# Attention and SwiGLU block with gradients: the forward loop staggered by one head, three weights transposed by DMA, the backward V loads issued earlier

## The chip, the cores and the metric

The kernel runs on one core of one Trainium2 chip. The core has five engines that run side by side, each in the order in which its own instructions were written: PE (matrix products), DVE (vector work), ACT (scalar work and copies), POOL (more vector work), and SP, which here only issues DMA transfers. Sixteen DMA engines move data between HBM and the on-chip memory. The metric is the device time of one execution in microseconds (us); lower is better.

## The reference

One decode step (batch 4, one token) of a pre-norm block, and its gradients. `_layernorm`, `_silu` and `_softmax` are the usual ones.

```python
def _A_ref(x, k_cache, v_cache, wq, wo):            # H=32 heads, Sk=4096, Dh=128
    q = (x @ wq).reshape(B, Sq, H, Dh).transpose(0, 2, 1, 3)
    p = softmax(einsum("bhqd,bhkd->bhqk", q, k_cache) * Dh ** -0.5)
    o = einsum("bhqk,bhkd->bhqd", p, v_cache)
    return o.transpose(0, 2, 1, 3).reshape(B, Sq, H * Dh) @ wo
def _B_ref(x, w1, w3, w2):                          # D=512, F=1792
    return (silu(x @ w1) * (x @ w3)) @ w2
h  = x + _A_ref(_layernorm(x), k_cache, v_cache, wq, wo)
h2 = h + _B_ref(_layernorm(h), w1, w3, w2)
out, vjp = jax.vjp(f, x, k_cache, v_cache, wq, wo, w1, w3, w2); grads = vjp(grad_out)
```

The outputs are `h2` and the gradients of x, k_cache, v_cache, wq, wo, w1, w3 and w2, in bf16. The two caches hold 128 heads (batch times heads) of 4096x128 values, 1 MB each; their gradients have the same size.

## The kernel before

**Forward.** The loop runs over 64 pairs of heads (`NGI` iterations `gi`, heads `a` and `b_`). For a pair, K is transposed (`T_pe`: one quarter of a head by PE with a copy by ACT, L309 and L310; `T_dve`: three quarters by DVE, L315), scores S are formed by PE (`S_head`, L341), and a softmax follows that passes between engines: row maximum on DVE (`mx` L348), a transpose on PE (`x_ps`), `gm` on DVE, a broadcast on PE (`b_ps`), `nm` on DVE, the exponential on ACT (`E`), the sum on PE (`l_ps` L379), its reciprocal on DVE (`rl` L384), the scaled copy `Pn` on ACT (L387), eight transposes of it on PE (`pt_P` L394) and four copies into `P_all` on ACT (L398). Then POOL writes the probabilities as pairs into a buffer PK (`PK_pairs` L404) and DVE multiplies K by them (`PK_mul` L408). In the next iteration PE forms the product M of V and PK over 32 blocks (`M_mm` L422), the sums `kP` (`M_end` L432) and ACT copies M out (L436). M and kP let the backward pass give the gradient of q without reading K again. Every eighth head ends a group: `wo_load` fetches 256 KB of wo and `attn` adds the attention output to `xr` (`at_ps` L461, L463).

**Buffers and queues.** All large tiles share 21 slots of 1 MB, given out in the order in which they were given back. K is loaded six heads ahead (`KQ`), V three (`VQ`), both by SP. SP's transfers use eight completion semaphores in turn, so an issue also waits until the eighth transfer before it has landed, and whatever stands behind it on SP waits too.

**Middle.** After the last head come the second layernorm (its root on ACT, L226), the products with w1 and w3 (`gu_ps`), the gate (`sigT` on ACT by Sigmoid, L709, and some DVE work), the product `dhn_ps` with w1 and w3 transposed (L724), the layernorm's gradient (L729 to L736), and the product `dOT_ps` with wo transposed (`woT`). The transposes of w1 and w3 (`wT_units`) and of wo (`woT_units`) are made by PE and copied out by ACT and DVE between the other steps; each weight is loaded once, as it lies in HBM.

**Backward.** For each of 128 heads V is loaded again and transposed (L928, L929), dP is formed (L933), and DVE forms the 1 MB gradients gv and gk as outer products (L940), which POOL and SP store. The loads of V for it (`load_V2`) begin in the middle; `prefetch` keeps up to seven ahead. The other gradients are worked off in small pieces beside it (`side_work`).

The core of the loop before:

```python
S_head(gi, 0); S_head(gi, 1); sm_max(gi)            # softmax of pair gi
M_mm(pa, ...)  ... sm_exp(gi) ... M_end(pa)         # M of the pair before
sm_sum(gi); sm_norm(gi)
M_mm(pb, 0, SJ); M_end(pb); load_V(pb + VQ)
T_pe(nb); sm_P(gi); PK_pairs(a); PK_pairs(b_)
PK_mul(a); T_dve(nb, 1..3); PK_mul(b_)
```

Of the kernel before, what the change touches and what calls it, by code (L numbers as in the profile page):

```python
# [9 lines left out]
FP32 = mybir.dt.float32  # L10
BF16 = mybir.dt.bfloat16
ALU = mybir.AluOpType
# [4 lines left out]
KQ = 6  # L17
# [8 lines left out]
def kernel(  # L26
# [116 lines left out]

    for s in range(KQ):
        load_K(s)
# [153 lines left out]
    hold = {}  # L299

# [105 lines left out]
    def PK_mul(s):  # L406
        PK = PKs[s].t[:].rearrange("p (j c) -> p j c", c=PKW)
        nc.vector.tensor_tensor(  # L408
            out=PK[:, :, 0:Dh].rearrange("p j (r t) -> p j r t", t=2),
            in0=Ks[s].heads().rearrange("p j (r t) -> p j r t", t=2),  # L410
            in1=PK[:, :, None, Dh:PKW].to_broadcast([P, SJ, Dh // 2, 2]),
            op=ALU.mult,
        )
        Ks.pop(s).give()

# [50 lines left out]
    def two_slots(nm):  # L466
        return [Slot(nm + "a"), Slot(nm + "b")]
# [7 lines left out]
    def load_w13(ap, nm):  # L475
        sl = two_slots(nm)
        for i in range(2):
            nc.sync.dma_start(out=sl[i].b(2 * F).rearrange("p (c f) -> p c f", c=2),
                              in_=ap[i * 2 * P:(i + 1) * 2 * P, :].rearrange("(c p) f -> p c f", p=P))
        return sl  # L480

# [38 lines left out]
    mid_w = {}  # L520

    def wT_units():
        for nm in ("w1", "w3"):
            w = mid_w[nm]
            wT = two_slots(nm + "T")
            mid_w[nm + "T"] = wT
            for f0 in range(0, FC, 2):
                pt = psT.tile([P, 2, DC, P], BF16, tag="tps", name="pt_w13")
                for i in range(2):
                    for cc in range(DC):  # L530
                        nc.tensor.transpose(pt[:, i, cc, :], w13_view(w, cc)[:, (f0 + i) * P:(f0 + i + 1) * P], ident_b[:])
                for i in range(2):
                    if (f0 // 7) == (f0 + 1) // 7:
                        if i == 0:
                            dst = wT[f0 // 7].b(7 * D).rearrange("p (c j) -> p c j", c=7)[:, f0 % 7:f0 % 7 + 2, :]
                            nc.scalar.copy(out=dst.rearrange("p a (n c) -> p a n c", c=P), in_=pt[:])
                    else:
                        nc.scalar.copy(out=w2_view(wT, f0 + i).rearrange("p (n c) -> p n c", c=P), in_=pt[:, i])
                yield

    units = {"d": d_hh_units(), "w": wT_units()}
# [13 lines left out]
    for gi in range(NGI + 1):  # L555
        fwd = gi < NGI
        last = gi >= NGI - 1
        a, b_ = gi * G, gi * G + 1
        pa, pb = a - 2, a - 1
        na, nb = a + 2, a + 3  # L560
        nxt = na < NH
# [7 lines left out]
        if gi > 0 and pb % 8 == 7:  # L569
            wo_load(pb)  # L570
        if gi > 0:
            M_mm(pa, 0, SJ // 2)
        if nxt:
            T_dve(na, 1)
        if fwd:
            sm_max_T(gi)
            sm_gmax(gi)
        if gi > 0:
            M_mm(pa, SJ // 2, SJ)
        if nxt:  # L580
            T_dve(na, 2)
        if fwd:
            sm_bcast(gi)
            sm_exp(gi)
        if gi > 0:
            M_end(pa)
            load_V(pa + VQ)
        if nxt:
            T_dve(na, 3)
        if fwd:  # L590
            sm_sum(gi)
            sm_norm(gi)
        if gi > 0:
            M_mm(pb, 0, SJ)
            M_end(pb)
            load_V(pb + VQ)
            if pb % 32 == 31:
                kP_flush(pb)
            if pb % 8 == 7:
                attn(pb)  # L600
        if nxt:
            T_pe(nb)
        if fwd:
            sm_P(gi)
            PK_pairs(a)
            PK_pairs(b_)
            PK_mul(a)
            load_K(a + KQ)
        if nxt:
            for c in range(NPE, 4):  # L610
                T_dve(nb, c)
        if fwd:
            PK_mul(b_)
            load_K(b_ + KQ)
        hold.pop(gi - 1, None)
        if 2 <= gi:
            step("d")
        if gi == NGI - 3:
            mid_w["w1"] = load_w13(B_w1, "w1")
        if gi == NGI - 2:  # L620
            mid_w["w3"] = load_w13(B_w3, "w3")
        if gi == NGI - 1:
            step("w", 7)
    step("w", 20)
# [20 lines left out]
    wo_pg = []  # L645

    def load_wo_page():
        pg = len(wo_pg)
        if pg < H // 8:
            wo_pg.append(Slot("wo8"))  # L650
            nc.sync.dma_start(out=wo_pg[pg].heads().rearrange("p j d -> p (j d)").rearrange("p (h j) -> p h j", h=8),
                              in_=A_wo[pg * 8 * P:(pg + 1) * 8 * P, :].rearrange("(h d) j -> d h j", d=P))

# [10 lines left out]
    with ExitStack() as cm:  # L664
# [3 lines left out]
        psWt = cm.enter_context(tc.tile_pool(name="psWt", bufs=4, space=bass.MemoryType.PSUM))  # L668
        for _ in range(4):
            load_wo_page()  # L670

# [4 lines left out]
        hhatT = mid.tile([P, DC, B], BF16, name="hhatT")  # L676
        rows_to_T(psA, hhatT[:], hhat, B, DC)
# [10 lines left out]
        woT = [Slot(f"woT{jj}") for jj in range(DC)]  # L688

        def woT_units():  # L690
            for pg in range(H // 8):
                for jj in range(DC):
                    pt = psWt.tile([P, GW, P], BF16, tag="wT", name="pt_wo")
                    src = wo_pg[pg].b(8 * D).rearrange("p (h j) -> p h j", h=8)
                    for hl in range(8):
                        nc.tensor.transpose(pt[:, hl, :], src[:, hl, jj * P:(jj + 1) * P], ident_b[:])
                    evac_copy(woT[jj].b(HD)[:, pg * 8 * P:(pg + 1) * 8 * P].rearrange("p (n c) -> p n c", c=P), pt[:],
                              eng="v" if jj == 3 else "s")
                    yield
                wo_pg[pg].give()  # L700

        units["o"] = woT_units()
# [6 lines left out]
        nc.scalar.activation(out=sigT[:], in_=gu_ps[:, 0], func=AF.Sigmoid)  # L709
        nc.vector.tensor_copy(out=gateT[:], in_=gu_ps[:, 0])  # L710
        nc.vector.tensor_copy(out=upT[:], in_=gu_ps[:, 1])
        step("o", 3)
# [15 lines left out]
        step("o", 4)  # L728
        nc.vector.tensor_copy(out=d_hn, in_=dhn_ps[:])  # L729
        for _ in range(3):  # L730
            load_V2()
        step("o", 5)
# [4 lines left out]
        step("o", 20)  # L737
# [7 lines left out]
        for h in range(H):  # L745
            for jj in range(DC):
                nc.tensor.matmul(dOT_ps[:, h, :], lhsT=woT[jj].b(HD)[:, h * Dh:(h + 1) * Dh], rhs=dhT[:, jj, :],
                                 start=(jj == 0), stop=(jj == DC - 1))
        for sl in woT:
            sl.give()  # L750
# [259 lines left out]
```

## Time and profile before

| | |
|---|---|
| time, median of 3 runs | 2164.55 us (2160.97 to 2164.81) |
| profiled execution: time, span | 2167.34 us, 2165.2 us |
| busy share of PE, DVE, ACT, POOL | 70%, 58%, 44%, 20% |
| bytes moved, mean rate | 712.01 MB, 329 GB/s |
| first and last row maximum of the forward | 23.3 us, 1045.9 us |
| first gradient product of the backward | 1108.14 us |

The span is the time from the first to the last instruction of the profiled execution; all places in the program below are given in us from its start. A row of the timeline gives start, duration, engine, line, operation, output and inputs, the number of instructions merged, and in brackets how long the engine had been idle and what ended that. PEclk is the granted share of the full TensorE clock, the DMA share the mean busy share of the sixteen DMA engines.

### The profile page before, as it was taken

To read this page: it belongs to the slowest core of one execution; us is meant where nothing else is said; L and a number is where in the kernel's file an instruction comes from. 1 tells how busy PE (TensorE), PEld (TensorE's weight loads), DVE (VectorE), ACT (ScalarE), POOL (GpSimd) and SP (SyncE) were. 2 spreads that over 40 slices of the span, in tenths; PEclk is the share of its full clock that TensorE was granted. 3 is DMA by queue.
4 is the path that set the end of the run, shared out by engine and by line. 5 is a ranking of instruction groups with operands and counts; after the bars stand their busy time and mean duration, and the time that the engine had idled before them with its cause. 6 is when DMAs were issued, how large, how long until landed. Compare 5 with 4: busy or idle time off the path is not lost.

```text
span 2165.2 us, 43701 instructions
## 1 busy us (share of the span) xinstructions
PE 1508.0 (70%) x18905; PEld 1212.3 (56%) x18905; DVE 1265.7 (58%) x1459; ACT 957.3 (44%) x1463; POOL 431.6 (20%) x665
## 2 busy tenths in 40 slices
PE   5767767777776776776788877686478658557553
PEld 4555555555555554555578875565366546446553
DVE  5556556556556556656356655475475666466665
ACT  2333322332232332232455555576377547546553
POOL 2121122122122112112011110121112222123232
PEclk8887887887788888788875666655565555556555
DMA  9876867677676776766589999899999999999998
GB/s 406 294 259 253 321 237 256 239 285 268 235 267 247 272 273 231 282 242 246 208 321 414 418 372 417 373 365 408 387 400 411 410 416 393 391 364 418 409 403 346
DMA packets 116400, 712.01 MB, mean 329 GB/s; under 512 B 11488, under 2 KB 29160, under 8 KB 33264
## 3 DMA queue, kind: packets, MB, share of 16 engines
q1 hardware_dynamic: 97520, 574.96, 69.1%
q0 software_dynamic: 18688, 134.28, 15.1%
q8 instruction: 147, 2.41, 0.4%
q14 instruction: 45, 0.37, 0.0%
HBM read 426.78 MB, written 282.34 MB: 328 GB/s over the span
## 4 chain that ended last, share of the span: by engine, by line
DMA 23%; PE 10%; ACT 9%; DVE 5%; issue 2%; SPq 1%; ACTq 0%; DVEq 0%
DMA out_dram<-gk 19%; ACT VT L929 7%; PE pt_tps L928 4%; DMA wq<-in_A_wq_dram 3%; DVE gv L940 2%; DVE gk L940 2%; PE dq_ps L781 2%; DMA w2a<-in_B_w_dram 1%; SPq L661 1%; PE dP_ps L933 1%; DMA out_dram<-gv 1%; PE gps L775 1%; PE rep_ps L912 1%; ACT rq L915 0%; ACT wqT L812 0%
## 5 line engine op out<-in xcount | busy, mean ns | idle before, releaser
L929 ACT COPY VT<-pt_tps 128x1024 bf16<-128x1024 bf16 x512 | 492.6, 1016 | 196.9 <-PE pt_tps L928 158.8
L928 PE MATMUL pt_tps<-ident_b,V 128*128 128x128 bf16 x4096 | 450.9, 293 | 114.7 <-ACT VT L929 114.7
L928 PEld LDWEIGHTS <-V 128*128 128x128 bf16 x4096 | 398.7, 137 | 174.8 <-issue 157.4
L408 DVE TENSOR_TENSOR PK<-Kn,PK 128x4096 bf16<-128x4096 bf16 x128 | 290.7, 2272 | 269.7 <-POOL PK L404 269.7
L940 DVE TENSOR_TENSOR gv<-P,rdo 128x4096 bf16<-128x4096 bf16 x128 | 293.7, 2295 | 171.6 <-DMA out_dram<-gk 144.8
L940 DVE TENSOR_TENSOR gk<-dS,rq 128x4096 bf16<-128x4096 bf16 x128 | 294.2, 2298 | 109.8 <-DMA out_dram<-gk 95.4
L422 PE MATMUL M_ps<-PK,Vn 128*128 128x130 bf16 x4096 | 344.8, 253 | 0.0
L310 ACT COPY KT<-pt_tps 128x1024 bf16<-128x1024 bf16 x128 | 129.4, 1012 | 468.6 <-PE pt_tps L309 446.7
L341 PE MATMUL S_ps<-KT,W 128*32 128x256 bf16 x1536 | 153.1, 345 | 253.9 <-DVE KT L315 253.9
L422 PEld LDWEIGHTS <-Vn 128*128 128x128 bf16 x4096 | 327.6, 118 | 3.9 <-issue 0.8
L315 DVE STREAM_TRANSPOSE KT<-Kn 128x512 f32<-128x512 f32 x384 | 254.7, 689 | 0.0
L952 POOL DMA_DIRECT2D out_dram<-gv x128 | 68.1, 532 | 837.2 <-DVE dSt L955 587.9
L933 PE MATMUL dP_ps<-dOT_bf,VT 128*128 128x1 bf16 x4096 | 150.2, 166 | 117.9 <-DVE dSt L955 59.2
L341 PEld LDWEIGHTS <-W 128*32 128x32 bf16 x1536 | 69.4, 107 | 287.2 <-issue 282.6
L933 PEld LDWEIGHTS <-VT 128*128 128x128 bf16 x4096 | 139.7, 103 | 132.2 <-ACT VT L929 69.0
L404 POOL COPY PK<-P_all 128x64 bf16<-128x64 bf16 x128 | 26.6, 241 | 819.0 <-ACT P_all L398 819.0
L321 POOL TENSOR_TENSOR W<-qrep,wmask 128x128 bf16<-128x128 bf16 x128 | 179.3, 1400 | 14.4 <-DVE qrep L272 14.4
L936 POOL COPY P<-P_all 128x64 bf16<-128x64 bf16 x128 | 140.7, 1099 | 0.0
L341 PE MATMUL S_ps<-KT,zq 128*32 128x256 bf16 x512 | 108.9, 332 | 4.0 <-ACT KT L310 0.3
L309 PEld LDWEIGHTS <-Kn 128*128 128x128 bf16 x1024 | 79.4, 120 | 54.1 <-issue 52.4
L309 PE MATMUL pt_tps<-ident_b,Kn 128*128 128x128 bf16 x1024 | 107.2, 268 | 0.7 <-DVE qrep L272 0.7
L373 ACT ACTIVATE E<-S_ps,nm 128x256 f32<-128x256 f32 x64 | 30.4, 474 | 173.9 <-DVE nm L370 173.9
(221 smaller groups left out, 1250.9 us busy)
## 6 DMA issues: line engine op xcount, KB each, us to landing
Kn<-in_A_k_cache_dram SPq DMA_DIRECT2D x128, 1024.0 KB, 5.1
Vn<-in_A_v_cache_dram SPq DMA_DIRECT2D x128, 1024.0 KB, 6.7
V<-in_A_v_cache_dram SPq DMA_DIRECT2D x128, 1024.0 KB, 21.8
out_dram<-gv POOLq DMA_DIRECT2D x128, 1024.0 KB, 11.2
out_dram<-gk SPq DMA_DIRECT2D x128, 1024.0 KB, 20.0
wq<-in_A_wq_dram SPq DMA_DIRECT2D x8, 1024.0 KB, 11.1
out_dram<-gw SPq DMA_DIRECT2D x6, 896.0 KB, 22.5
wo<-in_A_wo_dram SPq DMA_DIRECT2D x16, 256.0 KB, 6.4
```

The source lines that it names most:

```text
L309: nc.tensor.transpose(pt[:, i, :], Kn[:, c * GW + i, :], ident_b[:])
L310: nc.scalar.copy(out=KT[:, c * GW:(c + 1) * GW, :], in_=pt[:])
L315: nc.vector.transpose(out=KT[:, c * w_:(c + 1) * w_], in_=Kn[:, c * w_:(c + 1) * w_])
L321: nc.gpsimd.tensor_tensor(out=W[:, hl], in0=qrep[:, :, s:s + 1].to_broadcast([P, 4, 32]), in1=wmask[:, hl, None, :].to_broadcast([P, 4, 32 ...
L341: nc.tensor.matmul(st["S"][32 * c:32 * (c + 1), :], lhsT=lhsT, rhs=rhs, start=(hl == 0 and k == 0), stop=(hl == G - 1 and k == 3), tile_po ...
L408: nc.vector.tensor_tensor(out=PK[:, :, 0:Dh].rearrange("p j (r t) -> p j r t", t=2), in0=Ks[s].heads().rearrange("p j (r t) -> p j r t", t=2),
L422: nc.tensor.matmul(hold["M"][:], lhsT=Vn[:, j, :], rhs=PK[:, j, :], start=(j == 0), stop=(j == SJ - 1))
L928: nc.tensor.transpose(pt[:, i, :], Vn[:, g * GW + i, :], ident_b[:])
L929: nc.scalar.copy(out=VT[:, g * GW:(g + 1) * GW, :], in_=pt[:])
L933: nc.tensor.matmul(dP_ps[:, j:j + 1], lhsT=VT[:, j, :], rhs=dOT_bf[:, s:s + 1], start=True, stop=True)
L936: nc.gpsimd.tensor_copy(out=P2[:], in_=P_all[:, s, :, None].to_broadcast([P, SJ, 2]))
L940: nc.vector.tensor_tensor(out=dst.rearrange("p j (r t) -> p j r t", t=2), in0=col2[:, :, None, :].to_broadcast([P, SJ, Dh // 2, 2]), in1=r ...
```

## The change

The forward loop now works on heads that are one step apart: iteration `gi` does the softmax of heads a and a+1, the M products of heads a-3 and a-2, and the PK products of heads a-1 and a. So the PK product of head a-1, whose probabilities are from the iteration before, and two of DVE's transposes stand between `rl` and the PK product of head a. On PE 24 of the 32 M products of head a-2 stand between `l_ps` and the transposes of P; T of the second next head is ahead of `l_ps`. Two more iterations drain the loop. K is loaded 8 heads ahead (7 from head 80, 6 from head 96) by `more_K`, one head at a time. On DVE, one iteration in the middle of the forward, before (names: KT is K transposed, Kn is K as loaded):

```order
L384 RECIPROCAL rl<-l_ps 128x1
L408 TENSOR_TENSOR PK<-Kn,PK 128x32x128
L315 STREAM_TRANSPOSE KT<-Kn 128x512 x3
L408 TENSOR_TENSOR PK<-Kn,PK 128x32x128
L348 TENSOR_REDUCE mx<-S_ps 128x1
L350 TENSOR_SCALAR mxm<-maskneg,mx 128x2
L315 STREAM_TRANSPOSE KT<-Kn 128x512
L360 TENSOR_REDUCE gm<-x_ps 2x1
L315 STREAM_TRANSPOSE KT<-Kn 128x512
L370 COPY nm<-b_ps 128x1
L315 STREAM_TRANSPOSE KT<-Kn 128x512
```

and now, where the first product behind `rl` is that of head a-1 and the second that of head a:

```order
L393 RECIPROCAL rl<-l_ps 128x1
L417 TENSOR_TENSOR PK<-Kn,PK 128x32x128
L324 STREAM_TRANSPOSE KT<-Kn 128x512 x2
L417 TENSOR_TENSOR PK<-Kn,PK 128x32x128
L357 TENSOR_REDUCE mx<-S_ps 128x1
L359 TENSOR_SCALAR mxm<-maskneg,mx 128x2
L324 STREAM_TRANSPOSE KT<-Kn 128x512
L369 TENSOR_REDUCE gm<-x_ps 2x1
L324 STREAM_TRANSPOSE KT<-Kn 128x512
L379 COPY nm<-b_ps 128x1
L324 STREAM_TRANSPOSE KT<-Kn 128x512 x2
```

One transpose of the second head moved from behind the first PK product to ahead of the reciprocal, and the head that each product belongs to moved by one. On ACT, the same place before:

```order
L387 ACTIVATE Pn<-E,rl 128x1024
L436 COPY M<-M_ps 128x129
L443 COPY kP_sb<-kP_ps 128x512
L310 COPY KT<-pt_tps 128x1024
L398 COPY P_all<-pt_P 32x64 x4
```

and now (kP_sb stands only in every sixteenth iteration):

```order
L396 ACTIVATE Pn<-E,rl 128x1024
L407 COPY P_all<-pt_P 32x64 x4
L446 COPY M<-M_ps 128x129
L319 COPY KT<-pt_tps 128x1024
L382 ACTIVATE E,rs<-S_ps,nm 128x256
```

The copies into P_all stood behind an M copy and a KT copy and now stand right behind Pn.

In the middle, w3, w1 and wo are loaded a second time by eight transposing transfers (`DMA_TRANSPOSE`) of 0.9 to 1 MB, and PE, ACT and DVE make none of these transposes. `pump` issues the pending loads while slots are free, from the last iterations on. The order on SP from there, before (w1 and w3 were issued ahead of this; V is the second load of the V cache):

```order
L453 DMA wo_13293<-in_A_wo_dram 128x2x512
L651 DMA wo_13502<-in_A_wo_dram 128x8x512
L651 DMA wo_13504<-in_A_wo_dram 128x8x512
L651 DMA wo_13506<-in_A_wo_dram 128x8x512
L651 DMA wo_13508<-in_A_wo_dram 128x8x512
L661 DMA V_13760<-in_A_v_cache_dram 128x4096
```

and now, right behind the last V load of the forward and the four halves of w1 and w3:

```order
L535 DMA_TRANSPOSE w3T<-in_B_w_dram 128x7x512 x2
L535 DMA_TRANSPOSE w1T<-in_B_w_dram 128x7x512 x2
L540 DMA_TRANSPOSE woT<-in_A_wo_dram 128x4x1024
L463 DMA wo_13275<-in_A_wo_dram 128x2x512
L540 DMA_TRANSPOSE woT<-in_A_wo_dram 128x4x1024 x3
L675 DMA V_13503<-in_A_v_cache_dram 128x4096
```

The four plain loads of wo became eight transposing ones, and seven V loads follow them. The Sigmoid became an Exp with an addition and a reciprocal on DVE, and the ACT tables for the root and for Exp are called for early by a 1x1 activation on `warm`.

The diff, cut to its core:

```diff
-KQ = 6
...
+    def k_ahead(s):
+        return 8 if s < 80 else 7 if s < 96 else 6
+    def more_K(s):
+        while len(Ks) + kdone["n"] < min(NH, s + k_ahead(s)):
+            load_K(len(Ks) + kdone["n"])
...
+    def load_w13T_half(nm, ap, i):
+        sl = Slot(nm)
+        nc.sync.dma_start_transpose(out=sl.b(7 * D).rearrange("p (c j) -> p c j", c=7), in_=ap[:, i * 7 * P:(i + 1) * 7 * P])
+        mid_w[nm].append(sl)
+    def load_woT_page(pg):
+        sl = Slot("woT")
+        nc.sync.dma_start_transpose(out=sl.b(8 * D).rearrange("p (c n) -> p c n", c=DC), in_=A_wo[pg * 8 * P:(pg + 1) * 8 * P, :])
+        mid_w["woT"].append(sl)
+    def pump(reserve):
+        while pending and len(free) > reserve:
+            f_, *args = pending.popleft()
+            f_(*args)
...
-    for gi in range(NGI + 1):
+    for gi in range(NGI + 2):
         fwd = gi < NGI
+        m1, m2 = a - 3, a - 2
+        pk1 = a - 1
...
+        if has1:
+            if m1 % 8 == 7:
+                wo_load(m1)
+            M_mm(m1, 0, 16)
...
+            M_end(m1)
+            load_V(m1 + VQ)
+            if m1 % 8 == 7:
+                attn(m1)
+        if hasp:
+            PK_pairs(pk1)
         if nxt:
             T_dve(na, 3)
+            T_pe(nb)
+            T_dve(nb, 1)
         if fwd:
             sm_sum(gi)
             sm_norm(gi)
+        if hasp:
+            PK_mul(pk1)
+            more_K(pk1 + 1)
+        if has2:
+            M_mm(m2, 0, 24)
         if fwd:
             sm_P(gi)
+        if has2:
+            M_mm(m2, 24, SJ)
+            M_end(m2)
+            load_V(m2 + VQ)
+        if fwd:
             PK_pairs(a)
+        if nxt:
+            T_dve(nb, 2)
+            T_dve(nb, 3)
+        if fwd:
             PK_mul(a)
+            more_K(a + 1)
+        if gi >= NGI - 3:
+            pump(3 if gi < NGI - 1 else 2)
...
+        nc.scalar.activation(out=sigT[:], in_=gu_ps[:, 0], func=AF.Exp, scale=-1.0)
+        nc.vector.tensor_scalar(out=sigT[:], in0=sigT[:], scalar1=1.0, scalar2=None, op0=ALU.add)
+        nc.vector.reciprocal(out=sigT[:], in_=sigT[:])
```

More of the change, by code (lines that the diff above doesn't have):

```diff
@@ L667 @@
         psC = cm.enter_context(tc.tile_pool(name="psC", bufs=1, space=bass.MemoryType.PSUM))
-        psWt = cm.enter_context(tc.tile_pool(name="psWt", bufs=4, space=bass.MemoryType.PSUM))
-        for _ in range(4):
-            load_wo_page()
+        pump(1)
         hs = Slot("hhat")
@@ L687 @@
             sl.give()
[L688 to L702, printed above, removed]
+        pump(0)
+        assert not pending
+        while len(free) > 1:
+            load_V2()
         gateT = mid.tile([P, FC, B], FP32, name="gateT")
@@ L727 @@
             sl.give()
-        step("o", 4)
         nc.vector.tensor_copy(out=d_hn, in_=dhn_ps[:])
-        for _ in range(3):
+        while len(free) > 1:
             load_V2()
-        step("o", 5)
         lnb = mid.tile([B, D], FP32, name="lnb")
@@ L746 @@
             for jj in range(DC):
-                nc.tensor.matmul(dOT_ps[:, h, :], lhsT=woT[jj].b(HD)[:, h * Dh:(h + 1) * Dh], rhs=dhT[:, jj, :],
+                nc.tensor.matmul(dOT_ps[:, h, :], lhsT=mid_w["woT"][h // 8].b(8 * D).rearrange("p (c n) -> p c n", c=DC)[
+                    :, jj, (h % 8) * Dh:(h % 8 + 1) * Dh], rhs=dhT[:, jj, :],
                                  start=(jj == 0), stop=(jj == DC - 1))
-        for sl in woT:
+        for sl in mid_w["woT"]:
             sl.give()
```

118 lines of the change are left out of this document (37 added, 81 removed).

## The prediction

> **What bounds the kernel now.** I read the stretches first: which resource is full in the forward (23 to 1046 us), the middle (1064 to 1108) and the backward (1108 to the end). The columns are length, busy time of PE, weight load, DVE, ACT and POOL, granted PE clock, DMA share and GB/s.
>
> ```profile
> core 0: us, PE busy (x) PEld busy (x) DVE busy (x) ACT busy (x) POOL busy (x), PEclk, DMA share, GB/s
> 23.00:1046.00 1023.00, 734.08 (x8986) 553.62 (x8986) 598.35 (x855) 316.58 (x703) 214.50 (x374) 0.81 0.72 267
> 1064.00:1108.00 44.00, 32.80 (x497) 24.92 (x495) 12.97 (x44) 22.87 (x29) 1.97 (x5) 0.83 0.68 252
> 1108.00:2165.00 1057.00, 716.06 (x9019) 613.33 (x9017) 639.77 (x526) 604.37 (x709) 209.61 (x258) 0.58 0.98 395
> ```
>
> The backward is at a DMA share of 0.98: it takes as long as its bytes. In the forward nothing is full: PE 72%, DVE 58%, DMA 72%. So it is bound by a chain that passes between engines. The next rows are two waits of the whole run (total, times, longest) and the row maximum, once per pair:
>
> ```profile
> DVE PK L408 <- POOL PK L404: 269.7, 64, 5.0
> PE S_ps L341 <- DVE KT L315: 253.9, 189, 3.7
> L348 DVE TENSOR_REDUCE mx<-S_ps x64: 409/415/425, 23.3 to 1045.9; 128x1 f32<-128x256 f32 x64
> ```
>
> A pair takes (1045.9 - 23.3) / 63 = 16.23 us. In every one DVE waits 4.2 us (269.7 / 64) for the probabilities ahead of its PK product, and PE later waits for DVE's transposes. One pair on DVE, then the other engines from `rl` on:
>
> ```profile
> 508.36 0.42 DVE L348 TENSOR_REDUCE mx<-S_ps 128x1 f32<-128x256 f32 x1
> ...
> 512.28 0.17 DVE L384 RECIPROCAL rl<-l_ps 128x1 f32<-128x1 f32 x1 [0.45 <-PE l_ps L379]
> 517.37 2.29 DVE L408 TENSOR_TENSOR PK<-Kn,PK 128x4096 bf16<-128x4096 bf16 x1 [4.91 <-POOL PK L404]
> 519.58 1.89 DVE L315 STREAM_TRANSPOSE KT<-Kn 128x512 f32<-128x512 f32 x3
> 521.39 2.25 DVE L408 TENSOR_TENSOR PK<-Kn,PK 128x4096 bf16<-128x4096 bf16 x1
> 523.56 0.42 DVE L348 TENSOR_REDUCE mx<-S_ps 128x1 f32<-128x256 f32 x1
> ```
>
> ```profile
> 508.09 1.58 PE L422 MATMUL M_ps<-PK,Vn 128*128 128x130 bf16 x16
> 509.62 1.09 PE L422 MATMUL M_ps<-PK,Vn 128*128 128x130 bf16 x16
> 511.87 0.38 PE L379 MATMUL l_ps<-rs,bsum 128*128 128x1 f32 x2 [0.30 <-ACT E L373]
> 512.11 2.03 PE L422 MATMUL M_ps<-PK,Vn 128*128 128x130 bf16 x32
> 512.55 1.15 ACT L387 ACTIVATE Pn<-E,rl 128x1024 bf16<-128x1024 f32 x1 [0.58 <-DVE rl L384]
> 514.07 0.62 PE L432 MATMUL kP_ps<-PK,onesw 128*32 128x512 bf16 x8
> 514.62 0.62 PE L309 MATMUL pt_tps<-ident_b,Kn 128*128 128x128 bf16 x8
> 515.08 0.61 PE L394 MATMUL pt_P<-ident_b,Pn 128*128 128x128 bf16 x8
> 515.28 1.01 ACT L310 COPY KT<-pt_tps 128x1024 bf16<-128x1024 bf16 x1 [0.83 <-PE pt_tps L309]
> 516.19 0.84 ACT L398 COPY P_all<-pt_P 32x64 bf16<-32x64 bf16 x4
> 517.09 0.42 POOL L404 COPY PK<-P_all 128x64 bf16<-128x64 bf16 x2 [11.75 <-ACT P_all L398]
> 520.33 0.37 PE L341 MATMUL S_ps<-KT,W 128*32 128x256 bf16 x1 [3.72 <-DVE KT L315]
> ```
>
> This pair of 523.56 - 508.36 = 15.2 us is 4.1 from `mx` to the end of `rl`, 4.9 of DVE idle, and 6.2 of product, three transposes, product. In the idle time Pn ends at 513.70, but PE has 32 M products, kP and the transposes of K ahead of those of P (515.08), and ACT then the KT copy ahead of the copies into P_all.
>
> **The forward after the change.** Nothing in the loop is removed; it is put in another order. From `mx` to the end of `rl` I keep 4.1 us: DVE has one more transpose there (1.89 / 3 = 0.63), which fits into the waits. From `rl` the path to the product of head a is: hop 0.10, Pn 1.15, transposes to the first copy about 0.75 (K's: 514.62 to 515.28), P_all 0.84, POOL's first pair copy and hops 0.34 (516.19 + 0.84 to 517.37), 3.2 us together, and up to 0.5 more because the KT copy now stands ahead of Pn on ACT. DVE meanwhile does the product of a-1 (2.2, from 517.37 to 519.58) and two transposes (1.2): 3.4. So the wait of 4.9 shrinks to 0 to 0.3, say 0.2. Then the product of a, 2.2. One pair by compute: 4.1 + 3.4 + 0.2 + 2.2 = 9.9 us. What is late next is then the DMA: at 267 GB/s times 1023 us the forward moves 273 MB, 4.34 MB per pair. The rates at which saturated stretches ran:
>
> ```profile
> 20.00:40.00 20.00, 12.86 (x146) 8.93 (x145) 13.33 (x22) 8.44 (x13) 4.16 (x10) 0.74 1.01 426
> 40.00:60.00 20.00, 15.18 (x198) 11.39 (x198) 10.23 (x16) 7.01 (x16) 3.45 (x6) 0.83 1.01 412
> ```
>
> At 420 GB/s a pair's bytes need 10.3 us, at the backward's 395 they need 11.0. There is one cost in the new order. The load of wo is issued in the iteration that uses it, about 4 us ahead of `at_ps`; `at_ps` stands on PE ahead of everything that follows, and DVE waits for it at `xr`.
>
> ```profile
> wo<-in_A_wo_dram SPq DMA_DIRECT2D x16, 256.0 KB, 6.4
> w1a<-in_B_w_dram SPq DMA_DIRECT2D x1, 896.0 KB, 4.6
> Kn<-in_A_k_cache_dram SPq DMA_DIRECT2D x128, 1024.0 KB, 5.1
> dqflat<-dqr_bf SPq DMA_DIRECT2D x4, 8.0 KB, 2.4
> ```
>
> At the old landing time of 6.4 us that is a wait of 2.4 us in every fourth pair; behind a full queue of eight 1 MB loads at 2.5 us each it is 16. Between 0.6 and 4 us per pair, I take 1.1, nearer to the measured landing, since the loads ahead go on while the engines wait. Compute gives 9.9 + 1.1 = 11.0, as does the DMA at 395. So 11.0 us per pair: the last `mx` stands at 23.3 + 63 x 11.0 = 716 instead of 1045.9, a gain of 330. The bounds are 10.3 (44 us less) and, with the full price of wo, 13.9 (183 more).
>
> The Trainium skill has a rule against this. DMA: Bandwidth & Descriptors, section Specifications, limits a core's HBM traffic to about 358 GB/s, by which a pair would need an estimated 12.1 us. The rows above, 426 and 412 GB/s over 40 us, do not bear it out.
>
> **The middle.** Its rows, from the last M copy to the first gradient product:
>
> ```profile
> 1064.01 0.27 ACT L436 COPY M<-M_ps 128x129 f32<-128x129 f32 x1 [2.26 <-PE M_ps L422]
> 1075.95 0.15 DVE L227 RECIPROCAL rstd_h<-rstd_h 4x1 f32<-4x1 f32 x1 [6.90 <-ACT rstd_h L226]
> 1080.83 1.28 ACT L709 ACT_TABLE_LOAD   x1 [4.91 <-issue]
> L724 PE MATMUL dhn_ps<-w1Tb,d_gateT_bf x7: 379/379/379, 1089.2 to 1090.5; 128*4 128x512 bf16 x7
> 1096.04 0.66 DVE L235 TENSOR_SCALAR_CACHE_REDUCE lnb<-hhat 4x512 f32<-4x512 f32 x1
> 1103.82 0.29 DVE L751 CAST dOT_bf<-dOT_ps 128x128 bf16<-128x128 f32 x1 [2.72 <-PE dOT_ps L747]
> 1108.14 2.29 DVE L940 TENSOR_TENSOR gv<-P,rdo 128x4096 bf16<-128x4096 bf16 x1 [2.20 <-ACT rdo L915]
> ```
>
> Call the end of the last M copy T0 (1064.3). The last `mx` to T0 took 18.4 us with transposes of w1 in between; without them it is 4.1 to `rl`, 3.2 to the first product, two products of 2.2, 32 M products of 2.03 and hops: 14.3, a gain of 4. From T0 to the first product of the backward it took 43.8. The root on ACT waited behind copies of w3 (6.9, of which 0.2 stay: gain 6.7); the table load at 1080.83 goes ahead of time, while two small DVE operations come in (gain 0.9); wo's transposes and copies between `dhn_ps` (done at 1090.9) and the layernorm's gradient at 1096.04 go (0.7 us of copying stays: gain 4.4). So 31.8, if the weights are there. They come later than before: w1 and w3 (3.67 MB, 8.7 us at 420 GB/s) are issued at the end of iteration 63, about 5 us ahead of T0, and land near T0 + 4, in time for `gu_ps`. Behind them stand eight transposing loads, which no row shows. The low end is plain transfer at 420 GB/s: 7.86 MB in 18.7 us, all done at T0 + 23, in time for `dOT_ps` at about T0 + 24. The high end is the row for small pieces, 8 KB in 2.4 us: 270 to 310 us for each load. I take the nearest rows, plain loads of the same tiles from issue to landing, as if each waited for the one before it: 4 x 4.6 + 4 x 5.1 = 38.8, done at T0 + 43. `dOT_ps` is then 19 us late, and the middle takes 31.8 + 19 = 51 us, a loss of 7. The seven early V loads stand behind the transposes on SP, so the backward gets no head start: I leave its 1057 us.
>
> The Trainium skill disagrees with itself on such loads. Advanced Engine Details and Errata, section X-Bar Transpose (TRN2), calls them as fast as plain ones; DMA: Bandwidth & Descriptors, section Latency and other measured facts, measured 261 GB/s. By the latter the estimate is 30 us instead of 38.8 and the whole 9 us less than mine. No run here shows it yet.
>
> **Sum.** -330 - 4 + 7 = -327 on the profiled execution of 2167.3 gives 1840. That execution is 2.8 us above the median of 2164.55, so against the median I say 1838.
>
> **Rivals.** (1) PE becomes the bound. Per pair PE issues 64 M products (4.1 us at the clock of the row 512.11), and kP, the transposes of K and P, scores and small ones for roughly 4 more. At full clock 8.1 us hide beside 11.0. At the backward's granted 0.58 they would be 14.0, and the time 189 more: 2027. The slow rows exist (16 products in 1.58 us at 508.09 against 1.09 at 509.62). Against it: the slow ones come behind the 3.72 us wait for DVE, which goes, and even at the forward's mean of 0.81 it is 10.0. From about 0.74 on PE decides.
>
> By TensorE: Matmul & The Clock Gate, section Loop structure matters more than you think, an idle PE loses half its clock and a busy one gets it back; the trace's order of slow behind waiting agrees.
>
> (2) Transposing loads are slow, but not ruinous: at 20 us each the eight end at T0 + 166, `dOT_ps` is 142 late instead of 19, and the time is 1838 + 123 = 1961. For it speaks that each load turns 2-byte values around; against it only that it is one issue of a large size.
>
> (3) The other side: transposing loads at the price of small pieces. The gain of 327 is used up when the eight take about 327 us more than 39, some 46 us each; at 270 to 310 they would give near 4100. Slower from there on.
>
> (4) The reads do not keep 395 GB/s when PE, DVE and POOL work at the new pace. The page's slices of 54 us, busy tenths of the DMA engines and what they moved:
>
> ```profile
> DMA  9876867677676776766589999899999999999998
> GB/s 406 294 259 253 321 237 256 239 285 268 235 267 247 272 273 231 282 242 246 208 321 414 418 372 417 373 365 408 387 400 411 410 416 393 391 364 418 409 403 346
> ```
>
> Two slices of the backward with full DMA engines moved only 365 and 364. At 365 a pair takes 4.34 / 0.365 = 11.9 us, 0.9 more, and the time is 1838 + 57 = 1895. The page on DMA named above, by its 358 GB/s, would have it at an estimated 1907.
>
> (5) The wait only moves, because the product of head a-1 or its V is late in turn: 16.2 us per pair, and then with the loss of 7 and the gain of 4 in the middle 2168, no change. Against it, `PK_pairs` of a-1 needs only P_all of the iteration before.
>
> **Chances.** The forecast 0.57, (1) 0.15, (2) 0.12, (3) 0.04, (4) 0.07, (5) 0.03, and 0.02 for a forward at 10.3 us with plain-speed loads (1838 - 44 - 19 = 1775). A measurement of this kernel tells a change from none at about 0.2%, 4 us. Faster is everything but (3) and (5): 0.93; same 0.02; slower 0.05. The forecast's own range is 1785 to 1890. The range of 8 in 10 takes in (4) and (2) and a mild form of (1): 1785 to 1970.
>
> **What would show it.** Right: `mx` every 10 to 11.5 us and DVE's wait for POOL at PK under 1 us per pair; PEclk above 0.9 and DMA above 0.9 in the forward; the last `mx` near 716; a wait of `at_ps` for wo in every fourth pair; `dOT_ps` waiting for woT by about 19 us; the backward again 1057 us. Wrong: half-clock PE rows all through the forward (1), a wait for w3T of tens of us (2, 3), DMA share near 1 at under 380 GB/s (4), or DVE idle ahead of the first product behind `rl` (5).

## The result and the profile after

The changed kernel takes 1873.24 us (median of 4 runs, 1872.88 to 1875.13) against 2162.76 for the kernel before (4 runs beside them): a ratio of 0.8666, 95% interval 0.8649 to 0.8683. The prediction said 1838, range 1785 to 1970. The profiled execution has a span of 1873.3 us. Cut at the same four places as in the prediction, in us of the span:

| piece | before | predicted | after |
|---|---|---|---|
| start to first `mx` | 23.3 | 23.3 | 23.5 |
| first to last `mx` (63 pairs) | 1022.6 | 693 | 722.2 |
| last `mx` to T0, the end of the last M copy | 18.4 | 14.3 | 14.8 |
| T0 to the first gradient product | 43.8 | 51 | 56.6 |
| first gradient product to the end | 1057.1 | 1057 | 1056.2 |

The change took 35 us more than forecast, 29 of them in the forward and 6 in the middle. The stretches, with the columns as in the prediction (the last three are granted PE clock, DMA share, GB/s):

```profile
23.00:746.00 723.00, 570.24 (x8955) 462.89 (x8949) 595.01 (x854) 318.21 (x702) 215.21 (x374) 0.94 0.94 373
760.00:817.00 57.00, 21.65 (x317) 13.98 (x315) 10.94 (x41) 4.40 (x10) 1.88 (x5) 0.61 1.05 289
817.00:1873.00 1056.00, 718.38 (x9019) 616.70 (x9016) 640.11 (x526) 604.40 (x708) 211.54 (x258) 0.58 0.97 394
```

DVE's busy time in the forward is nearly what it was, 595 us against 598, now in 723 us instead of 1023: 82% instead of 58%. The clock rose from 0.81 to 0.94, the bytes from 267 to 373 GB/s. The row maximum and the three waits that matter, over the whole run (total, times, longest):

```profile
L357 DVE TENSOR_REDUCE mx<-S_ps x64: 407/411/424, 23.5 to 745.7; 128x1 f32<-128x256 f32 x64
DVE PK L417 <- POOL PK L413: 28.9, 59, 3.1
DVE xr L473 <- PE at_ps L471: 86.4, 16, 21.4
PE at_ps L471 <- DMA wo<-in_A_wo_dram: 80.4, 15, 20.6
```

DVE's wait for the probabilities fell from 269.7 to 28.9 us. In its place `at_ps` waits for wo, 80.4 us in all, which DVE passes on at `xr`. In a pair without `attn`, DVE looks like this:

```profile
510.87 0.15 DVE L393 RECIPROCAL rl<-l_ps 128x1 f32<-128x1 f32 x1
510.93 2.29 DVE L417 TENSOR_TENSOR PK<-Kn,PK 128x4096 bf16<-128x4096 bf16 x1
513.14 1.30 DVE L324 STREAM_TRANSPOSE KT<-Kn 128x512 f32<-128x512 f32 x2
514.90 2.47 DVE L417 TENSOR_TENSOR PK<-Kn,PK 128x4096 bf16<-128x4096 bf16 x1 [0.47 <-POOL PK L413]
517.29 0.41 DVE L357 TENSOR_REDUCE mx<-S_ps 128x1 f32<-128x256 f32 x1
```

Behind `rl` stand the product of head a-1 and two transposes, and only 0.47 us of waiting is left of 4.91. The next `mx` starts at 527.29: 10.0 us, where 9.9 were predicted.

### The profile page after: what moved, and what is told of

It reads as the page before. It is cut to its first block, busy times and chain, and to the rows that moved or that the text cites. A ratio compares the mean times of both kernels' runs of the same rounds, so it can differ in the third digit from the quotient of the medians.

```text
span 1873.3 us, 43348 instructions
## 1 busy us (share of the span) xinstructions
PE 1332.1 (71%) x18665; PEld 1111.3 (59%) x18665; DVE 1262.7 (67%) x1456; ACT 935.6 (50%) x1438; POOL 434.2 (23%) x666
## 4 chain that ended last, share of the span: by engine, by line
DMA 31%; PE 10%; ACT 8%; DVE 8%; issue 4%; SPq 2%; POOL 0%; ACTq 0%; DVEq 0%; POOLq 0%
DMA out_dram<-gk 23%; ACT VT L930 7%; PE pt_tps L929 4%; DVE gv L941 3%; DVE gk L941 3%; DMA out_dram<-gw 2%; DMA wq<-in_A_wq_dram 2%; PE dq_ps L782 2%; DMA w2a<-in_B_w_dram 1%; DVE PK L417 1%; SPq L675 1%; PE dP_ps L934 1%; DMA wo<-in_A_wo_dram 1%; DMA out_dram<-gv 1%; SPq L535 1%
## 5 line engine op out<-in xcount | busy, mean ns | idle before, releaser
L417 DVE TENSOR_TENSOR PK<-Kn,PK 128x4096 bf16<-128x4096 bf16 x128 | 302.7, 2366 | 28.9 <-POOL PK L413 28.9
L432 PE MATMUL M_ps<-PK,Vn 128*128 128x130 bf16 x4096 | 298.9, 228 | 2.5 <-DMA Vn<-in_A_v_cache_dram 1.7
L432 PEld LDWEIGHTS <-Vn 128*128 128x128 bf16 x4096 | 270.4, 103 | 18.9 <-issue 16.4
L332 POOL COPY zq<-qT_bf 128x2 bf16<-128x2 bf16 x128 | 152.2, 1189 | 0.0
L956 DVE TENSOR_SCALAR dSt<-dP_ps,c_rep 128x32 f32<-128x32 f32 x128 | 31.4, 245 | 90.1 <-PE dP_ps L934 90.1
L318 PE MATMUL pt_tps<-ident_b,Kn 128*128 128x128 bf16 x1024 | 84.8, 230 | 1.9 <-DMA Kn<-in_A_k_cache_dram 1.2
L318 PEld LDWEIGHTS <-Kn 128*128 128x128 bf16 x1024 | 65.0, 103 | 33.0 <-issue 25.9
L407 ACT COPY P_all<-pt_P 32x64 bf16<-32x64 bf16 x256 | 52.1, 203 | 59.0 <-PE pt_P L403 56.7
L442 PE MATMUL kP_ps<-PK,onesw 128*32 128x512 bf16 x1024 | 79.4, 387 | 0.0
```

The lines of the kernel that those rows point to most:

```text
L318: nc.tensor.transpose(pt[:, i, :], Kn[:, c * GW + i, :], ident_b[:])
L332: nc.gpsimd.tensor_copy(out=zq[gi % 2][hl][:, 32:132:67], in_=qT_bf[:, s:s + 1].to_broadcast([P, 2]))
L417: nc.vector.tensor_tensor(out=PK[:, :, 0:Dh].rearrange("p j (r t) -> p j r t", t=2), in0=Ks[s].heads().rearrange("p j (r t) -> p j r t", t=2),
L432: nc.tensor.matmul(hold["M"][:], lhsT=Vn[:, j, :], rhs=PK[:, j, :], start=(j == 0), stop=(j == SJ - 1))
L442: nc.tensor.matmul(hold["kP"][32 * q:32 * (q + 1), :, :], lhsT=ones_window(w), rhs=PK[:, j0:j0 + 4, 0:Dh], start=(w == 0 and c == 0), stop ...
```

## The experiments

Each ratio is to the kernel before, run beside the version on the same chip. Differences to the change in us are between medians of different groups of runs; the kernel before took 2161 to 2165 us in them.

**wo four pairs early.** The load of wo is issued half a group ahead of its use.

```diff
-            if m1 % 8 == 7:
-                wo_load(m1)
+            if m1 % 8 == 3:
+                wo_load(m1 + 4)
```

> The changed kernel, but each 256 KB load of wo is issued two iterations (four heads) before attn uses it; nothing else moves. Theory: the new late work of the forward is at_ps waiting for a wo load that is issued about 4 us ahead of its use into a full queue. Then every fourth pair, now 14 to 18.7 us, falls to about 11, the mean pair from 11.46 to about 10.4 (the DMA floor of 4.34 MB at 420 GB/s), the last mx from 745.7 to about 680, and the middle loses about 11 us too, since its own wo load no longer stands behind five transposing loads: about 1873 - 67 - 11 = 1795. Rival: the forward is held by the rate of the DMA engines, 375 GB/s in this trace; then the pairs stay at 11.5 on average (the fourth ones shorter, the others longer) and only the middle gains: about 1862.

Measured: 1806.82 us (1806.36 to 1814.45), ratio 0.8362 (0.8329 to 0.8395). The theory's figure was 12 us too good; the rival's 1862 is ruled out. Forward stretch and row maximum of this kernel:

```profile
23.00:685.00 662.00, 550.08 (x8958) 441.32 (x8950) 593.48 (x855) 318.09 (x702) 215.19 (x374) 0.98 1.00 407
L357 DVE TENSOR_REDUCE mx<-S_ps x64: 408/411/425, 23.6 to 684.5; 128x1 f32<-128x256 f32 x64
```

The last `mx` comes 61.2 us earlier, the middle is 16.7 shorter (39.8), the backward 9.5 longer (1065.7). A pair takes 10.49 us on the mean, at a DMA share of 1.00 and 407 GB/s over 662 us. One cost of the group's output is left, and no row of it is a wait for wo. DVE in a pair in which `attn` runs:

```profile
496.62 0.16 DVE L379 COPY nm<-b_ps 128x1 f32<-128x1 f32 x1 [0.22 <-PE b_ps L374]
497.57 0.17 DVE L467 CAST o<-M 128x8 bf16<-128x8 f32 x1 [0.79 <-ACT M L446]
498.42 0.68 DVE L473 TENSOR_TENSOR xr<-xr,at_ps 4x512 f32<-4x512 f32 x1 [0.69 <-PE at_ps L471]
499.03 1.28 DVE L324 STREAM_TRANSPOSE KT<-Kn 128x512 f32<-128x512 f32 x2
500.25 0.12 DVE L393 RECIPROCAL rl<-l_ps 128x1 f32<-128x1 f32 x1
```

In the next pair, without `attn`, `nm` starts at 508.39 and the two transposes at 508.46, 0.07 us behind it; here they start 2.41 us behind it, and `rl` with them. This pair took 11.8 us, its neighbours 10.0. On the mean the 15 pairs with `attn` take 12.15 us and the 48 without it 9.97; three of the 15, in which kP is written out too, take 13.5 to 14.8.

**Only the last group's wo early.**

```diff
-            if m1 % 8 == 7:
-                wo_load(m1)
+            if m1 % 8 == 7 and m1 != NH - 1 or m1 == NH - 5:
+                wo_load(m1 // 8 * 8 + 7)
```

> The changed kernel with only the last of the sixteen wo loads issued two iterations earlier, ahead of the transposing loads on SP. Theory: at_ps of the last group waits 20.6 us because its load is issued only when SP has issued five transposing loads at 4 to 5 us each. Without that wait the next thing late is woT, whose last load is issued about 10 us before dOT_ps now needs it: gain about 11, 1862. Rival: nothing else is late, gain 20, 1853. Other rival: the middle waits for the landing of the weights and not for the issue, gain 0.

Measured: 1867.74 us (1864.56 to 1872.53), ratio 0.8639 (0.8601 to 0.8678); the interval overlaps that of the change itself, so the time alone decides nothing. The trace does:

```profile
763.77 0.59 PE L471 MATMUL at_ps<-wo,o 128*4 128x512 bf16 x2 [0.36 <-DVE o L467]
796.76 1.01 PE L747 MATMUL dOT_ps<-dhT,woT 128*128 128x4 bf16 x32 [2.89 <-DMA woT<-in_A_wo_dram]
794.70 4.42 SPq L675 DMA_DIRECT2D V<-in_A_v_cache_dram  x8
```

`at_ps` no longer waits and runs 19 us earlier, `dOT_ps` now waits 6.5 us in three pieces for woT, and the first gradient product comes at 802.0 instead of 817.1. The whole gained 5.5 us by the medians, not the theory's 11. Seven of the 15 us are lost again in the backward (1062.9 instead of 1056.2). The V loads are issued at 794.7, as late as before (793.9), because the transposing loads still stand ahead of them on SP. That this is the reason is likely but not shown: in five kernels whose V loads begin 20 to 23 us ahead of the first gradient product, the backward varied from 1050 to 1062 without it.

**Plain loads in place of transposing ones** (the kernel leaves the transposition out of the four loads of w3 and w1 and the four of wo; the sizes are the same).

```diff
-        nc.sync.dma_start_transpose(out=sl.b(7 * D)..., in_=ap[:, i * 7 * P:(i + 1) * 7 * P])
+        nc.sync.dma_start(out=sl.b(7 * D).rearrange("p (c f) -> p c f", c=4), in_=...)
...
-        nc.sync.dma_start_transpose(out=sl.b(8 * D)..., in_=A_wo[pg * 8 * P:(pg + 1) * 8 * P, :])
+        nc.sync.dma_start(out=sl.b(8 * D).rearrange("p (h j) -> p h j", h=8), in_=...)
```

> The changed kernel with the eight transposing loads of w3T, w1T and woT replaced by plain loads of the same bytes into the same slots, so that w3T, w1T and woT hold untransposed values; everything else as it is. Theory: a transposing load costs SP 4 to 5 us of issue, and so holds the wo load, the other weights and the V loads behind it. With plain issues of 0.4 us the eight are bound by their bytes, wo lands near 768 instead of 783, and the time falls by about 15 to 1858. Rival: the bytes cost the time, not the issue; then no gain beyond 3 us.

Measured: 1871.36 us (1864.38 to 1873.39), ratio 0.8646 (0.8613 to 0.868): not told apart from the change.

```profile
756.65 3.50 SPq L535 DMA_DIRECT2D w3T<-in_B_w_dram  x2
760.25 4.11 SPq L535 DMA_DIRECT2D w1T<-in_B_w_dram  x2
766.67 4.62 SPq L463 DMA_DIRECT2D wo<-in_A_wo_dram  x1
778.95 1.01 PE L471 MATMUL at_ps<-wo,o 128*4 128x512 bf16 x2 [12.17 <-DMA wo<-in_A_wo_dram]
```

The wait for the last wo fell from 20.6 to 12.2, and the middle from 56.6 to 48.5. Here the last `mx` came 4.2 us later than in the change (749.9 against 745.7, with the same code up to there; it lies between 743.0 and 749.9 in the runs that share it), which hides half of that. What transposing costs beyond a plain load in this place is therefore about 8 us of the middle; the rest of the wait comes of standing behind full loads on SP. The theory's 15 us did not come: wo landed near 779, not 768. The stretch in which SP issues these loads, in the change (from the second transposing load on) and here:

```profile
762.40:793.90 31.50, 5.96 (x123) 4.15 (x123) 4.79 (x18) 2.11 (x5) 0.91 (x2) 0.56 1.11 227
756.60:786.00 29.40, 12.55 (x220) 9.88 (x220) 7.29 (x11) 3.85 (x11) 1.02 (x3) 0.72 1.06 369
```

The DMA engines are full in both, but they move 227 GB/s with the transposing loads and 369 with plain ones. At 227 GB/s 0.92 and 1.05 MB need an estimated 4.0 and 4.6 us, which is what SP spends on issuing one. So the theory's reading, that the issue costs the time, is not shown: the issue may only last as long as the bytes move, and no run tells the two apart.

**Depth of K in the kernel before.**

```diff
-    for s in range(KQ):
-        load_K(s)
+    def k_ahead(s):
+        return 8 if s < 80 else 7 if s < 96 else 6
...
-            load_K(a + KQ)
+            more_K(a + 1)
```

> The kernel before with only its K loads changed to run 8, 7 and 6 heads ahead as in the changed kernel. Theory: the gain comes from the order of the work, and K was never late before (DMA share 0.72): no change, 2162 within 5. Rival: the deeper K prefetch makes a part of the gain: faster by more than 20.

Measured: 2160.92 us (2152.64 to 2169.09, 10 runs), ratio 0.9992 (0.9971 to 1.0013). Alone, the deeper queue does nothing.

**The cover taken away.** The product of head a-1 goes back ahead of `l_ps` and `rl`.

```diff
+        if hasp:
+            PK_mul(pk1)
+            more_K(pk1 + 1)
         if fwd:
             sm_sum(gi)
             sm_norm(gi)
...
-        if hasp:
-            PK_mul(pk1)
-            more_K(pk1 + 1)
```

> The changed kernel with one thing moved: the PK product of head a-1 stands ahead of l_ps and rl again, so that it no longer covers the way from rl to the product of head a. Theory (the forward is bound by the chain, and the cover of 3.4 us is the gain): DVE's first product of 2.2 us ends later than exp does, so rl starts about 2 us later, and behind rl only two transposes of 1.2 us cover 3.2 us of Pn, transposes, P_all and pair copy. About +2.0 us per pair, part of it against the wo wait: +90 to +130, so 1965 to 2005. DVE's wait for POOL at PK rises from 0.4 to over 1.5 us per pair. Rival (the forward is now bound by the DMA, the chain has room): within +40 of 1873.

Measured: 1962.03 us (1956.18 to 1963.81), ratio 0.906 (0.9038 to 0.9083), 89 us over the change: the theory, 3 us below its range. DVE in one pair:

```profile
516.56 2.25 DVE L417 TENSOR_TENSOR PK<-Kn,PK 128x4096 bf16<-128x4096 bf16 x1
518.73 0.16 DVE L393 RECIPROCAL rl<-l_ps 128x1 f32<-128x1 f32 x1
518.81 1.28 DVE L324 STREAM_TRANSPOSE KT<-Kn 128x512 f32<-128x512 f32 x2
522.23 2.47 DVE L417 TENSOR_TENSOR PK<-Kn,PK 128x4096 bf16<-128x4096 bf16 x1 [2.14 <-POOL PK L413]
524.63 0.41 DVE L357 TENSOR_REDUCE mx<-S_ps 128x1 f32<-128x256 f32 x1
```

The wait is 2.14 instead of 0.47, and the pair (524.63 less 512.99) 11.64 instead of 10.0. The whole run's wait is 148.2 us in 64 pairs, 2.3 each. In return the waits for wo shrink, 36.7 us in 8 times instead of 80.4 in 15.

**All M products of head m2 ahead of P.** The last 8 of the 32 products, kP and the M copy go ahead of the transposes and copies of P.

```diff
-            M_mm(m2, 0, 24)
-        if fwd:
-            sm_P(gi)
-        if has2:
-            M_mm(m2, 24, SJ)
+            M_mm(m2, 0, SJ)
             M_end(m2)
             load_V(m2 + VQ)
+        if fwd:
+            sm_P(gi)
```

> The changed kernel with the last 8 of the 32 M products of head m2, kP, and the M copy put ahead of the transposes and copies of P, as the kernel before had it. Theory (the way from rl to the product of a is on the path): 8 M products of 0.5 us, 8 kP products of 0.6 and an M copy of 0.3 stand ahead of it, and the cover has 0.2 to spare: about +1 us per pair, 1920 to 1940, shown as DVE waiting for POOL at PK about 1.2 us per pair. Rival (DMA-bound, or PE's queue runs ahead anyway): within 10 us of 1873.

Measured: 1891.67 us (1889.66 to 1899.95), ratio 0.8751 (0.8721 to 0.8781), 18 us over the change: neither figure. The mechanism is the theory's, the size is not:

```profile
DVE PK L417 <- POOL PK L413: 58.2, 63, 2.7
L357 DVE TENSOR_REDUCE mx<-S_ps x64: 406/411/425, 23.5 to 769.9; 128x1 f32<-128x256 f32 x64
```

The wait at PK doubles, from 0.45 to 0.91 us per pair, and a pair takes 11.85 instead of 11.46 us. I had charged the moved work in full, 1.4 us, but part of it runs while PE would wait for Pn anyway: 0.61 us in a pair of the change.

**V loads of the backward issued later in the program.**

```diff
         assert not pending
-        while len(free) > 1:
-            load_V2()
...
-        while len(free) > 1:
-            load_V2()
```

> The changed kernel without the two loops that issue V loads of the backward in the middle; the first V loads are then issued where the backward begins in the program. Theory: SP's queue holds nothing but loads, so it comes to them as soon as the transposing loads are issued wherever they stand in the program; one load less goes ahead (7 instead of 8). Within 6 us of 1873, first V load still issued at about 794. Rival (the early issue is a gain of its own: 8 loads at 2.5 us that run beside the middle): +15 to +20, about 1890.

Measured: 1878.33 us (1874.69 to 1883.38), ratio 0.868 (0.8657 to 0.8703), overlapping the change's. SP issues the V loads at the same time and just as many of them:

```profile
791.82 10.28 SPq L675 DMA_DIRECT2D V<-in_A_v_cache_dram  x8
```

(My count of seven, here and ahead of the prediction, was off by one.) Where these loads stand in the program is of no weight: SP has nothing else to do and comes to them as soon as the loads ahead are issued. So the earlier issue of the V loads, the third part of the change, gains nothing by itself.

**Transposing loads on ACT's queue**, on top of wo four pairs early.

```diff
-        nc.sync.dma_start_transpose(...)
+        nc.scalar.dma_start_transpose(...)
```

> The version with every load of wo four pairs early (1806.8), and the eight transposing loads issued on ACT's queue instead of SP's. Theory (each such issue holds its queue for 4 to 5 us, whatever queue it is): SP is free 40 us earlier, V loads start as soon as slots come free, about 20 us earlier, but five issues of 4 to 5 us now stand on ACT ahead of the layernorm's root, about 20 us on the path from the last M copy to the first gradient product: 1800 to 1825, with rstd_h waiting about 20 us. Rival (the issue costs ACT nothing, the time on SP was a wait for the loads in flight): 1780 to 1795.

Measured: 1820.6 us (1814.91 to 1823.27), ratio 0.8408 (0.8385 to 0.8431), against 0.8362 with SP (0.8329 to 0.8395): no better, probably worse. ACT's queue, and SP's V loads:

```profile
705.73 4.06 ACTq L535 DMA_TRANSPOSE w3T<-in_B_w_dram  x1
735.69 0.20 ACT L233 ACTIVATE rstd_h<-rstd_h 4x1 f32<-4x1 f32 x1 [12.76 <-issue]
739.16 14.42 SPq L675 DMA_DIRECT2D V<-in_A_v_cache_dram  x8
```

The time lies in the theory's range, but it came about in another way. Behind the first, which took 11.7 us, an issue takes 3.9 to 4.6 us on ACT too, so it is the transposing load and not the queue. ACT's copies of M, and then the root, stand behind it: the root came 7.8 us late, not 20, but the copies had lost 27 us before, so that T0 came 35.3 us behind the last `mx` instead of 14.8. The backward was 18 us shorter in return (1047.6 against 1065.7). And the V loads did not start 20 us earlier but 7 us later (731.8 with SP): they wait for slots that w1 and w3 give back late. That part of the theory was wrong.

**Six loads of K ahead in the changed kernel, and in the version with wo early.**

```diff
-        return 8 if s < 80 else 7 if s < 96 else 6
+        return 6
```

> The changed kernel with 6 loads of K ahead throughout instead of 8, 7 and 6. Theory (pair of 9.9 by compute plus a wait for wo; the DMA has room at 373 GB/s): two loads less to fall back on cost nothing, 1873 plus or minus 10. Second reading (the wait for wo is long because many loads are in flight ahead of it): with fewer loads ahead the wait shrinks from about 6 us in every fourth pair to 3 to 4, 1835 to 1850. Rival (the depth is part of the gain): the reads stop during the wo wait and K comes late after it, over 1890.

> The version with every load of wo four pairs early (1806.8), with 6 loads of K ahead throughout. Theory (that version runs at 407 GB/s with DMA share 1.00, a queue that never runs empty): the depth changes nothing, 1807 plus or minus 8. Rival (at this rate the depth carries the stretches in which the engines fall behind): K late at the transposes, over 1820.

Measured: 1851.27 us (1846.76 to 1852.09), ratio 0.8564 (0.8538 to 0.8589), 22 us under the change; and 1802.18 us (1799.96 to 1805.03), ratio 0.8344 (0.8324 to 0.8365), not told apart from 0.8362. The theory's "nothing" is right for the second and wrong for the first. The second reading nearly has the time, but not the reason: wo lands later, not sooner (10.0 us median against 8.6). It is issued sooner. The same group in the change and with six ahead, SP and then DVE, the change first:

```profile
353.37 0.33 SPq L136 DMA_DIRECT2D Kn<-in_A_k_cache_dram  x1
353.74 0.43 SPq L463 DMA_DIRECT2D wo<-in_A_wo_dram  x1
355.89 0.41 DVE L357 TENSOR_REDUCE mx<-S_ps 128x1 f32<-128x256 f32 x1
362.73 0.68 DVE L473 TENSOR_TENSOR xr<-xr,at_ps 4x512 f32<-4x512 f32 x1 [3.44 <-PE at_ps L471]
```

```profile
329.32 0.33 SPq L136 DMA_DIRECT2D Kn<-in_A_k_cache_dram  x1
329.70 0.43 SPq L463 DMA_DIRECT2D wo<-in_A_wo_dram  x1
337.13 0.41 DVE L357 TENSOR_REDUCE mx<-S_ps 128x1 f32<-128x256 f32 x1
341.28 0.68 DVE L473 TENSOR_TENSOR xr<-xr,at_ps 4x512 f32<-4x512 f32 x1 [0.69 <-PE at_ps L471]
```

In both, wo follows at once on a K load that SP had to hold until a slot was free, for 3.5 us with eight ahead and 3.4 with six. But with eight that is 2.2 us ahead of `mx`, with six 7.4. Over the 15 groups of the forward the mean lead is 4.1 instead of 2.6 us, and `xr` follows 7.2 instead of 8.1 us behind `mx`: 13 of the 22 us. Of the other 9, about 6 lie in the pairs without `attn` (9.86 instead of 9.99 us on the mean); why those are shorter, and why the K load gets its slot sooner, no run settles.

## Why the prediction was right or wrong, point by point

**A pair by compute, 9.9 us: right, and for the reason given.** Of the 48 pairs without `attn`, 44 take 9.6 to 10.1 us. The terms are off by a little each and cancel: 3.7 us from `mx` to the end of `rl` instead of 4.1, 3.4 as forecast, 0.5 of waiting instead of 0.2, and 2.4 for the product instead of 2.2. The way from 15.2 is shown by the cover experiment: without the cover a pair takes 11.6, so the cover gives 1.6 of the 5.2. The other 3.6 are, by the rows, 1.6 for the shorter way from `rl` to the product of a (4.9 before, 3.3 in that experiment; the order of M and P, tried by itself, is 0.4 of it) and 1.9 for the transposes that stood between the two products and now run in the softmax's waits. These two were not tried apart.

**wo, 1.1 us per pair: the term that was too small.** It held the wait and left out the output that wo is loaded for. Beyond 9.9 a pair takes 1.56 more on the mean (722.2 / 63 less 9.9): pairs with `attn` average 16.19, those without 9.99. The wait that I priced is 59.8 us between 50 and 740, 0.95 per pair, even less than I took. What I left out, `attn` itself, with wo in place still holds DVE's transposes, and with them `rl`, for 1.8 us in every fourth pair, 0.44 per pair, because my 9.9 was read from a pair that has none. Together 1.39. Of the remaining 0.17, an estimated 0.11 are the three pairs that also write out kP, as the version with wo early has them, and 0.07 the pairs without `attn`, 9.99 instead of 9.9. The kernel before hid a part of this. There `attn` stood behind `rl`, inside the wait for the probabilities that the change takes away, and made it only 0.6 us longer (5.5 from the end of `rl` to the product at 420.98); the change put it ahead of `rl`. DVE in such a pair before:

```profile
415.29 0.17 DVE L384 RECIPROCAL rl<-l_ps 128x1 f32<-128x1 f32 x1 [0.45 <-PE l_ps L379]
418.34 0.67 DVE L463 TENSOR_TENSOR xr<-xr,at_ps 4x512 f32<-4x512 f32 x1 [0.69 <-PE at_ps L461]
```

The step that failed is "from `mx` to the end of `rl` I keep 4.1 us": with `attn` it is 6.0 even when wo is there (494.33 to 500.37 in the version with wo early). The rows of the kernel before had a hint of it: the pair that I read took 15.2 us, the mean pair 16.23. Loading wo early takes away the wait and leaves `attn`, and 10.49 us per pair is what came of it.

The low bound on the rate, 10.3 us per pair at 420 GB/s, was nearly reached there, 10.49 at 407. The Trainium skill's page DMA: Bandwidth & Descriptors, section Specifications, with its limit of about 358 GB/s for a core, is not borne out by that row.

**Last `mx` to T0: 14.8 for 14.3, right.**

**The middle: 56.6 for 51, near, by another mechanism.** The steps themselves came near what I had worked out: with the last wo early the middle takes 40.6 us, 34.1 without its wait for woT, against 31.8. But the transposing loads delay something else than I said. SP, the M copy that ends T0, and what follows:

```profile
752.40 14.06 SPq L535 DMA_TRANSPOSE w3T<-in_B_w_dram  x2
766.56 8.22 SPq L535 DMA_TRANSPOSE w1T<-in_B_w_dram  x2
774.87 4.72 SPq L540 DMA_TRANSPOSE woT<-in_A_wo_dram  x1
779.64 0.57 SPq L463 DMA_DIRECT2D wo<-in_A_wo_dram  x1
780.32 13.53 SPq L540 DMA_TRANSPOSE woT<-in_A_wo_dram  x3
793.94 10.56 SPq L675 DMA_DIRECT2D V<-in_A_v_cache_dram  x8
```

```profile
760.25 0.27 ACT L446 COPY M<-M_ps 128x129 f32<-128x129 f32 x1 [2.26 <-PE M_ps L432]
783.15 1.01 PE L471 MATMUL at_ps<-wo,o 128*4 128x512 bf16 x2 [20.62 <-DMA wo<-in_A_wo_dram]
817.08 2.29 DVE L941 TENSOR_TENSOR gv<-P,rdo 128x4096 bf16<-128x4096 bf16 x1 [2.11 <-ACT rdo L916]
```

The last group's wo, 256 KB, stands on SP behind five transposing loads, each of which holds the queue for 4 to 5 us, and `at_ps` waits 20.6 us for it. The first holds it for 9.9 us and ends 1.1 us after the last plain load ahead of it has landed (761.2), so it is probably held by the loads in flight. By the time `dOT_ps` comes, woT is there. I had placed the lateness at `dOT_ps`, 19 us, from landing times. The eight do follow one another, in 41.5 us from the first issue to the end of the last against my 38.8. That this is so near is partly luck: I had taken 4.6 and 5.1 us from the landing of plain loads, which is not what spaces transposing ones (4 to 5 us each, at 227 GB/s with the DMA engines full). The step that failed is that I followed what is late behind the transposing loads only to woT and V, and not to the wo load that the order puts among them. The experiment on the last wo shows both: with wo early, `dOT_ps` waits for woT, as I had said, but only 6.5 us.

On the disagreement of the Trainium skill about such loads: Advanced Engine Details and Errata, section X-Bar Transpose (TRN2), calls them as fast as plain ones, which 227 against 369 GB/s does not bear out. The 261 GB/s of the Trainium skill's page DMA: Bandwidth & Descriptors, section Latency and other measured facts, is nearer to the 227 of this trace, in which one 256 KB load is among them.

**The backward: 1056.2 for 1057, right.** Across the experiments it took 1048 to 1066 from the first gradient product. The three longest, 1063 to 1066, are those in which that product came 7 us behind the first V load instead of 19 or more; no run tests this alone.

**The rivals.** PE as the bound (1) fell at a granted 0.94 in the forward. Slow transposing loads (2, 3) fell: where the change's trace tells, they land 6.4 to 7.7 us after issue, and one follows the other after 4 to 5. (By its own terms (2) ends at T0 + 164, not 166, and comes to 1959.) Reads that do not keep up (4) fell with 407 GB/s in the version with wo early. A wait that only moves (5) fell at 0.45 us per pair, though a new wait did come in for wo.

## What to carry to other kernels

When a chain is shortened, look for what was free only because the chain was long: here a 256 KB load issued just ahead of its use, and a small product that a typical pair does not contain; price the pair that has them, not only the one that has not. A small load that an engine waits for is issued where nothing that waits for a slot, and nothing that is slow to issue, stands ahead of it on its queue: moving one line was worth another 66 us here (0.8362 against 0.8666). And cover is proved by taking it away: 2.2 us of other work put behind a wait was worth 1.6.

## What the runs showed of the hardware

Landing times grow with the rate at which the DMA engines run. The same loads took, in the kernel before, 5.1 (K) and 6.4 us (wo), at 267 GB/s, and now, at 373:

```profile
Kn<-in_A_k_cache_dram SPq DMA_DIRECT2D x128, 1024.0 KB, 9.0
wo<-in_A_wo_dram SPq DMA_DIRECT2D x16, 256.0 KB, 8.6
```

A transposing load of 0.9 to 1 MB holds the queue that issues it, here for 3.9 to 4.8 us on SP and 3.9 to 4.6 on ACT, apart from the first (9.9 and 11.7); a plain one of 1 MB takes 0.33 us where nothing is in its way. The transposing ones moved 227 GB/s with the DMA engines full, plain ones in their place 369. And more loads ahead can cost time: with eight of K instead of six, the K load that stands ahead of wo on SP got its slot later, and wo, behind it, came 1.5 us later on the mean against `mx`.
